# Attention decode with a gated MLP: VectorE's next product ahead of its last step on the maxima, and K's buffer signalled from an earlier matmul

## The chip, the cores and the metric

The kernel runs on one core of a Trainium2 chip. The metric is the device time in microseconds (us); lower is better. Engines are TensorE (PE, with its weight loads as PEld), VectorE (DVE), ScalarE (ACT), GpSimd (POOL) and SyncE (SP), which issues nearly all transfers. Data come from HBM through 16 DMA engines.

## The reference

One decoding step for two tokens with a long K and V cache, beside a small MLP whose output gates the attention's. All in float32.

```python
B, Sq, D = 2, 1, 512;  H, Sk, Dh = 32, 8192, 128;  F = 1376
xn = layernorm(x)
q = (xn @ wq)                                   # (B, H, 1, Dh)
scores = einsum("bhqd,bhkd->bhqk", q, k_cache) * Dh ** -0.5
o = einsum("bhqk,bhkd->bhqd", softmax(scores), v_cache)
s = o.reshape(B, 1, H * Dh) @ wo
h = gelu(layernorm(xn) @ w1 + b1)
g = silu(h @ w2 + b2)
return x + s * g
```

K and V are 2 x 32 heads x 8192 x 128 float32 each, so some 537 MB are read, against a few MB of weights.

## The kernel before, in words

Each of the 64 (token, head) heads has an 8192 x 128 K and V. Two heads make one **pair**: 64 partitions each, 128 rows of the cache on every partition. So there are N = 32 pairs, numbered 0 to 31, and a pair's K or V is one transfer of 128 x 16384 float32, 8 MiB. Three buffers of that size fill the memory: `KBUF[0]` and `KBUF[1]` for K by turns, and one `VB` for V. (All three carry the name `big` in the profile.) The weights of the set-up and at the end the output weights `wo` lie in the same buffers.

For each pair n:

- VectorE waits for the pair's q row (`s_q`, two accumulators in PSUM by turns) and for K (`d_k0` or `d_k1`), and multiplies K in place by q: the **product** (`TENSOR_TENSOR big<-big,bank`). It sums each row into 128 scores a partition: `TENSOR_REDUCE sc<-big`. The **maxima** of each partition come next: `TENSOR_REDUCE MX<-sc`, signal `v_mx`.
- TensorE transposes the row of maxima (`bank<-ident,MX`, signal `p_m`), and VectorE's **last step**, `TENSOR_REDUCE nm<-bank`, takes the largest of each head with its sign turned (signal `v_nm`).
- TensorE spreads the two numbers over the partitions with two small matmuls (`bank<-nm,srow`). The first gives K's buffer back (`p_k`), the second (`p_n`) sends ScalarE on: it copies the bias, takes two exponentials into `PZ` (signal `s_pz`) and writes the q of two pairs later (`s_q`).
- The **V stage**: TensorE waits for `s_pz` and for V (`d_v`), then runs 32 matmuls with V (`bank<-big,PZ`), ScalarE copies the result to `o4`, and eight matmuls collect it. The first of them gives `VB` back (`p_free`).
- `unread(...)` are matmuls whose results nobody reads; some stand between the others on TensorE.

SP issues transfers in an order written out by hand. In the middle it takes `p_k` and issues the K of two pairs later, then takes `p_free` and issues the next V, in turn, so that the queue holds K, V, K, V. The last K, the last V and `wo` are cut into pieces. On each engine a loop over the pairs (two to a turn on VectorE, ScalarE and SP) runs by itself, and `take` (line 45) is a wait on a semaphore that also counts it down. Most instructions of the program are recorded by one helper, so that they carry line 51.

At the start, K0 is loaded early, K1 after the q projection has been read from its buffer, and V0 once the whole set-up is done.

Of the kernel before, what the change touches and what calls it, by code (L numbers as in the profile page):

```python
# [5 lines left out]
ALU = mybir.AluOpType  # L6
AX = mybir.AxisListType
# [6 lines left out]
class Program:  # L14
# [28 lines left out]
    def take(self, eng, name, v=1):  # L43

        self.engines[eng].wait_ge(self.sem(name), v).then_inc(self.sem(name), -v)  # L45

    def op(self, eng, method, *args, waits=(), sig=None, by=1, quiet=False, **kwargs):
        need = self.need(eng, waits)
        for name, v in need[:-1]:
            self.engines[eng].wait_ge(self.sem(name), v)  # L50
        ins = getattr(self.engines[eng], method)(*args, **kwargs)  # L51
        for name, v in need[-1:]:
            ins._wait_ge(self.sem(name), v)
        if quiet:
            return None
        name = sig or "own_" + eng
        by = 16 if method == "dma_start" else by
        ins.then_inc(self.sem(name), by)
        self.counts[name] += by
        return name, self.counts[name]  # L60


def decode_kernel(nc, x, kc, vc, wq, wo, w1, b1, w2, b2, out):
    P = 128
    B, H, S, DH = kc.shape
# [3 lines left out]
    U = 2  # L69
    HP = P // U  # L70
    KP = S // HP
# [21 lines left out]
    HALVES = (0, KP // 2, KP)  # L93

    pr = Program(nc)
    op, wait, take = pr.op, pr.wait, pr.take

    def sb(shape, name):
        return nc.alloc_sbuf_tensor(name, list(shape), F32).ap()

    def ps(shape, name):
        return nc.alloc_psum_tensor(name, list(shape), F32).ap()
# [6 lines left out]
    KBUF, VB = rows[:2], rows[2]  # L109
# [24 lines left out]
    Q = sb([P, N + U, DH], "Q")  # L134
    ident = sb([P, P], "ident")
    ones = sb([P, B], "ones")
    srow = sb([1, HP], "srow")
# [18 lines left out]
    SC = [sb([P, KP], f"sc{i}") for i in range(2)]  # L156
    MX = sb([P, 1], "MX")
    nm = sb([1, U], "nm")
# [11 lines left out]
    bank = [ps([P, 512], f"bank{i}") for i in range(8)]  # L170
    po = bank[0]
    pm = bank[1]
    pn = bank[1][:, 2 * P:]
# [4 lines left out]
    pq2 = [bank[2][:, :DH], bank[7][:, :DH]]  # L178
# [8 lines left out]
    QH = len(PB) // 2  # L187
# [6 lines left out]
    def pe_n(name, n):  # L194
        return name, n + 1

    t = {}
# [31 lines left out]
    for k in (7, 6, 1, 2, 4, 0):  # L229
# [13 lines left out]
                  op=ALU.add)  # L243
    t["sel"] = op("DVE", "tensor_copy",
                  sel[:, HP:].rearrange("p (b j r) -> p b j r", b=B, r=HG)[:, :, :QT, 0], by_row[:, :B, :],
                  waits=[t["sel0"]])
# [36 lines left out]
    for part, n0, n1 in (("first", 0, NPB), ("rest", NPB, N)):  # L283
        shape = [BH, n1 - n0, DH]
        t[f"QN {part}"] = op("DVE", "tensor_tensor", out=QN[:, n0:n1, :], in0=q_all.unsqueeze(1).to_broadcast(shape),
                           in1=mine[:, n0:n1].unsqueeze(2).to_broadcast(shape), op=ALU.mult,
                           waits=[t["qall"], t["mine"]])
# [15 lines left out]
    for b in range(B):  # L303
        t["x4"] = op("SP", "dma_start", x4[HB * b::R, :], x[b, 0].rearrange("(j n) -> j n", n=P), sig="d_x4",
                     waits=[t["x4m"]])
# [23 lines left out]
            op("SP", "dma_start", wo_sb[:, c0:c1, n0:n1], wo_v[:, c0:c1, n0:n1], sig=f"d_wo{i}" if not h else "d_wol")  # L329


    def scores(u, q, sems, cuts):
        k = KBUF[u]
        for name, (c0, c1) in zip(sems, zip(cuts, cuts[1:])):
            take("DVE", name, 16)
            op("DVE", "tensor_tensor", out=k[:, c0:c1], in0=k[:, c0:c1],
               in1=q.unsqueeze(1).to_broadcast([P, c1 - c0, DH]), op=ALU.mult, sig="v_t")
            take("DVE", "v_t")
            op("DVE", "tensor_reduce", out=SC[u][:, c0:c1], in_=k[:, c0:c1], axis=AX.X, op=ALU.add, sig="v_r")
        take("DVE", "v_r", len(sems))  # L340
        op("DVE", "tensor_reduce", out=MX, in_=SC[u], axis=AX.X, op=ALU.max, sig="v_mx")
        take("DVE", "p_m")
        op("DVE", "tensor_reduce", out=nm, in_=pm[:1, :P].rearrange("o (s r) -> o s r", s=U), axis=AX.X,
           op=ALU.max, negate=True, sig="v_nm")

    with nc.vector.Fori(0, N // U - 1) as i:
        for u in range(U):
            take("DVE", "s_q")
            scores(u, pq2[u], [f"d_k{u}"], (0, KP))
    for u in range(U):  # L350
        take("DVE", "s_q")
        scores(u, pq2[u], ["d_k1", "d_kl"] if u else ["d_k0"], HALVES if u else (0, KP))


    with nc.scalar.Fori(0, N // U) as i:
        for u in range(U):
# [4 lines left out]
            for s in range(U):  # L361
# [11 lines left out]
                   waits=[t["th"], t["pool"]])  # L373
    shape = [P, N, U * PH]
    t["ZL"] = op("DVE", "tensor_tensor", out=ZL, in0=half.unsqueeze(1).to_broadcast(shape),
                 in1=RS.unsqueeze(2).to_broadcast(shape), op=ALU.mult, waits=[pe_n("p_z", 0), t["half"]])
# [3 lines left out]
                in1=OT.unsqueeze(2).to_broadcast(shape), op=ALU.mult, waits=[t["OT"], t["blk"]])  # L380
    t["on"] = op("DVE", "tensor_tensor", out=on[:, ::HB, :], in0=OA[:, :, :OC], in1=rl.unsqueeze(2).to_broadcast([P, B, OC]),
                 op=ALU.mult, waits=[t["rl"], t["on0"], pe_n("p_oa", 0)])
    t["wide"] = op("ACT", "copy", o4, pw, waits=[pe_n("p_w", 0)])
    a = op("DVE", "scalar_tensor_tensor", res, acc, 0.5, gate, op0=ALU.mult, op1=ALU.mult,
           waits=[pe_n("p_acc", 0), t["gate"]])
    t["res"] = op("DVE", "tensor_add", res, res, x4, waits=[a, t["x4"]])
    t["out"] = op("SP", "dma_start", out.rearrange("b s (j n) -> j (b s) n", n=P), res[::HB, :], sig="d_out",
                  waits=[t["res"]])
# [6 lines left out]
    def mm(dst, w, v, start=True, stop=True, sig=None, waits=(), skip=False):  # L395
        kw = {"skip_group_check": True} if skip else {}
        if sig in PE_EVENTS:
            done.append(sig)
            sig = "pe_setup"
        return op("PE", "matmul", dst, w, v, start=start, stop=stop, waits=waits, sig=sig, quiet=sig is None, **kw)  # L400
# [15 lines left out]
    for c in range(ND):  # L416
# [4 lines left out]
        j, k = NF % QT, NF // QT  # L421
# [6 lines left out]
    j, k = NF % QT, NF // QT  # L428
    mm(ph[R * j:R * j + B, k * P:k * P + FT], ones[:1, :B], b1_sb[:, NF * P:], start=False, stop=True, sig="ph")
    by_tile = ident.rearrange("p (j r) -> p j r", r=R)  # L430
    for k in range(NH):
        n = min(QT, NF + 1 - k * QT)
        mm(phT[:, k * QT * B:(k * QT + n) * B].rearrange("p (j b) -> p j b", b=B), h_nat[:, k * P:(k + 1) * P],
           by_tile[:, :n, :B], waits=[t["h"]], sig="phT" if k == NH - 1 else None)
    for n in range(NG // QT):
        for c in range(ND):
            for j in range(QT):
                g = n * QT + j
# [3 lines left out]
    for n in range(NG // QT):  # L442
        for hh in range(HG):
# [3 lines left out]
               waits=[t["sel"], t["qnat"]], sig="pqa" if last else None)  # L447

    for g in range(N // NPB):
        mm(PB[g % len(PB)], sides, QN[:, g * NPB:(g + 1) * NPB, :].rearrange("h n d -> h (n d)"),  # L450
           waits=[t["side"], t["QN rest" if g else "QN first"]] + ([t[f"Q{QH}"]] if g >= len(PB) else []),
           sig=f"pb{g}")
    for f in range(NF + 1):
        j = f % QT
        k = P if f < NF else FT
        mm(pg[R * j:R * j + B, :], hT[:k, f, :], w2_sb[:k, f, :], start=f < QT, stop=f + QT > NF and j != QT - 1,
           waits=[t["hT"], t["w2"], t["mem6"]])
    mm(pg[R * (QT - 1):R * (QT - 1) + B, :], ones[:1, :B], b2_sb, start=False, stop=True, waits=[t["b2"]], sig="pg")
    for j in range(QT):
        mm(pgate[R * j:R * j + MB, :], mod_b[:, :MB], g_nat[:, j * P:(j + 1) * P], waits=[t["g"], t["mod_b"]],  # L460
           sig="pgate" if j == QT - 1 else None)
    assert done == PE_EVENTS, done

    def unread(*heads):

        for n in heads:
            mm(bank[6][:, :n * DH], ident, Q[:, :n, :].rearrange("p n d -> p (n d)"), waits=[t["g"], t[f"Q{QH}"]])

    def softmax(first=False):
        if not first:  # L470
            unread(4, 4)
        take("PE", "v_mx")
        op("PE", "transpose", pm[:1, :P], MX, ident, sig="p_m")
        if not first:
            unread(1)
        take("PE", "v_nm")
        for s in range(U):
            mm(pn[HP * s:HP * (s + 1), :1], srow, nm[:, s:s + 1], sig="p_n" if s == U - 1 else "p_k")

    def weighted(v, last=False):  # L480
        if last:
            unread(4, 2)
        take("PE", "s_pz")
        if not last:
            take("PE", "d_v", 16)
        for i in range(NT):
            if last and i * JW == HALVES[1]:
                unread(2)
            if last and i * JW in HALVES:
                nc.tensor.wait_ge(pr.sem(f"d_v31{HALVES.index(i * JW)}"), 16)  # L490
            j = i % QT
            mm(po[R * j:R * j + U * JW, :], PZ[:, i].rearrange("p s j -> p (s j)"),
               v[:, i * JW:(i + 1) * JW, :].rearrange("p j d -> p (j d)"), start=i < QT, stop=i + QT >= NT,
               sig="p_v" if i == NT - 1 else "p_z" if last and i == 0 else None)
        if last:
            for b in range(B):
                m = slice(b * HH, (b + 1) * HH)
                mm(OA[:, b, OC:], ZL[:, m].rearrange("p n r -> p (n r)"), ones[:, :1], waits=[t["ZL"]],
                   sig="p_den" if b == B - 1 else None)
            unread(1)  # L500
        take("PE", "s_o4")
        for i in range(JW):
            mm(pt[:, :U], o4[:, i * DH:(i + 1) * DH], mod[:, i:U * JW:JW], start=i == 0, stop=i == JW - 1,
               sig="p_t" if i == JW - 1 else "p_free" if i == 0 else None)

    wait("PE", t["mem"], t["pool"], t["mod"], t["z"])
    softmax(first=True)
    with nc.tensor.Fori(0, N - 1):
        weighted(VB)
        softmax()  # L510
# [15 lines left out]
    for b in range(B):  # L526
        h = slice(b * H, (b + 1) * H)
        mm(OA[:, b, :OC], Z[:, h].rearrange("p h r -> p (h r)"), mod, waits=[t["Z"]],
           sig="p_oa" if b == B - 1 else None)
    unread(1)  # L530
    for i, (c0, c1) in enumerate(zip(WO_CUTS, WO_CUTS[1:])):
        for c in range(c0, c1):
            after = [t["on"], t["mem"], (f"d_wo{i}", 16)]
            if c < WIDE:
                j = c % QT
                mm(pw[R * j:R * j + MB, :], on[:, :, c], wo_sb[:, c, :], start=c < QT, stop=c + QT >= WIDE,
                   waits=after, sig="p_w" if c == WIDE - 1 else None)
# [7 lines left out]
        if c1 == OC - 2:  # L545
            for j in range(QT):
                mm(acc[R * j:R * j + MB, :], mod[:, :MB], o4[:, j * P:(j + 1) * P], start=False, stop=False,
                   waits=[t["wide"]])
# [26 lines left out]
```

## Time and profile before

| | |
|---|---|
| median of 3 runs | 1300.71 us (1299.7 to 1301.15) |
| the profiled execution's own time | 1299.53 us |
| its span, first to last instruction | 1298.2 us |
| VectorE busy | 1135.7 us, 87% |
| TensorE busy | 465.6 us, 36% |
| ScalarE busy | 81.1 us, 6% |
| moved from HBM | 559.30 MB, 431 GB/s over the span |

Busy times are sums over the span. The profile's numbers are those of one execution, whose time differs a little from the median.

### The profile page before, as it was taken

How to read it: one execution, taken by the hardware profiler on the slowest of the kernel's cores; microseconds unless marked ns; L12 is line 12 of the kernel's file. 1: busy time of each engine (PE TensorE's matmuls, PEld its weight loads, DVE VectorE, ACT ScalarE, POOL GpSimd, SP SyncE). 2: the span in 40 equal slices, each digit the busy share in tenths (PEclk: the TensorE clock that was granted, in tenths of full speed). 3: DMA queues.
4: the chain of work that ended last, by engine and by line, in shares of the span. 5: the costliest groups of instructions: out<-in, count | busy, mean ns of one | idle time of the engine just before them, and what ended most of it. 6: DMA issues, size and time to landing. Idle time of an engine off the chain costs nothing. (4 is left out here: it accounts for less than half of the span.)

```text
span 1298.2 us, 7420 instructions
## 1 busy us (share of the span) xinstructions
PE 465.6 (36%) x2958; PEld 150.8 (12%) x2958; DVE 1135.7 (87%) x171; ACT 81.1 (6%) x279; POOL 2.3 (0%) x15
## 2 busy tenths in 40 slices
PE   3813343323334322433322343322334321333338
PEld 1201111001111000111100111100111100111103
DVE  2599999988889988889988888988888988888991
ACT  1200000000000000000000000000000000000000
POOL 0000000000000000000000000000000000000000
PEclk8757766666776566677656767656776666677659
DMA  9999999999999999999999999999999999999998
GB/s 412 436 426 442 430 430 436 426 446 426 438 430 424 446 426 442 430 430 436 426 446 426 438 430 424 446 426 444 428 432 434 426 446 426 438 430 424 432 436 360
DMA packets 11241, 559.37 MB, mean 431 GB/s; under 512 B 1264, under 2 KB 1536, under 8 KB 1892
## 3 DMA queue, kind: packets, MB, share of 16 engines
q1 hardware_dynamic: 11228, 559.30, 99.7%
q8 instruction: 3, 0.05, 0.0%
q14 instruction: 2, 0.02, 0.0%
q10 hardware_dynamic: 8, 0.01, 0.0%
HBM read 559.30 MB, written 0.00 MB: 431 GB/s over the span
## 5 line engine op out<-in xcount | busy, mean ns | idle before, releaser
L51 DVE TENSOR_TENSOR big<-big,bank 128x16384 f32<-128x16384 f32 (+1 forms) x33 | 551.2, 16704 | 73.2 <-DVEq L45 73.2
L51 DVE TENSOR_REDUCE sc<-big 128x128 f32<-128x16384 f32 (+1 forms) x33 | 551.2, 16703 | 4.8
L51 PE MATMUL bank<-big,PZ 128*8 128x512 f32 x2048 | 293.0, 736 | 632.1 <-PEq L45 632.1
L51 PEld LDWEIGHTS bank<-big,PZ 128*8 128x8 f32 x2048 | 60.5, 103 | 837.3 <-issue 837.3
L51 PE MATMUL bank<-Q,ident 128*128 128x512 f32 (+2 forms) x198 | 79.8, 514 | 0.3 <-issue 0.3
L51 ACT COPY o<-bank 128x512 f32<-128x512 f32 x33 | 19.3, 586 | 887.3 <-ACTq L45 875.9
L51 PE MATMUL bank<-ident,MX 128*1 128x128 f32 x32 | 9.8, 308 | 132.8 <-PEq L45 132.8
L51 PE MATMUL bank<-mod,o 128*128 128x2 f32 x256 | 32.8, 250 | 27.4 <-PEq L45 27.4
L51 PEld LDWEIGHTS bank<-mod,o 128*128 128x128 f32 x256 | 31.0, 191 | 55.4 <-issue 55.4
L51 PEld LDWEIGHTS bank<-Q,ident 128*128 128x128 f32 x198 | 34.8, 205 | 16.5 <-issue 16.5
L51 ACT ACTIVATE PZ<-sc,bias 64x128 f32<-64x128 f32 x64 | 25.5, 399 | 6.6 <-ACTq L45 6.2
L51 DVE TENSOR_REDUCE nm<-bank 1x2 f32<-1x128 f32 x32 | 8.9, 279 | 19.4 <-DVEq L45 19.4
L51 DVE TENSOR_TENSOR big<-big,mine 64x512 f32<-64x512 f32 (+1 forms) x2 | 4.5, 2278 | 21.2 <-ACT big L51 21.2
L51 PEld LDWEIGHTS bank<-ident,MX 128*1 128x1 f32 x32 | 2.5, 79 | 157.8 <-issue 157.8
L51 ACT COPY bias<-bank 128x1 f32<-128x1 f32 x32 | 5.1, 159 | 220.2 <-ACTq L45 220.2
L51 PE MATMUL bank<-big,sides 64*128 64x512 f32 x16 | 12.8, 972 | 3.7 <-DVE big L51 3.7
L51 PE MATMUL bank<-nm,srow 1*64 1x1 f32 x128 | 10.4, 218 | 8.9 <-PEq L45 7.1
L51 DVE TENSOR_REDUCE MX<-sc 128x1 f32<-128x128 f32 x32 | 9.2, 286 | 4.7
L51 PE MATMUL bank<-big,xnT 128*2 128x512 f32 x64 | 9.0, 727 | 10.3 <-DMA big<-in_A_wq_dram 10.3
L51 ACT ACTIVATION_READ_ACCUMULATOR PZ<-sc,bias x64 | 11.8, 185 | 0.0
L51 PE MATMUL bank<-big,on 128*17 128x512 f32 (+1 forms) x88 | 10.8, 569 | 0.9 <-DMA big<-in_A_wo_dram 0.8
L51 DVE SCALAR_TENSOR_TENSOR res<-bank,gate 128x128 f32<-128x128 f32 x1 | 0.3, 291 | 11.9 <-PE bank L51 11.9
(80 smaller groups left out, 83.8 us busy)
## 6 DMA issues: line engine op xcount, KB each, us to landing
big<-in_A_k_cache_dram SPq DMA_DIRECT2D x2, 4096.0 KB, 35.9
big<-in_A_v_cache_dram SPq DMA_DIRECT2D x2, 4096.0 KB, 35.8
big<-in_B_w_dram SPq DMA_DIRECT2D x1, 2752.0 KB, 10.2
big<-in_B_w_dram SPq DMA_DIRECT2D x1, 2560.0 KB, 52.1
big<-in_A_wo_dram SPq DMA_DIRECT2D x1, 2560.0 KB, 15.0
big<-in_A_wo_dram SPq DMA_DIRECT2D x1, 2048.0 KB, 19.5
big<-in_A_wo_dram SPq DMA_DIRECT2D x1, 1536.0 KB, 22.7
big<-in_A_wo_dram SPq DMA_DIRECT2D x1, 1024.0 KB, 24.8
```

Of the source, the lines that this page charges most:

```text
L51: ins = getattr(self.engines[eng], method)(*args, **kwargs)
```

## The change

On VectorE the function `scores`, which did all steps of one pair, is cut into `product`, `total`, `maxima` and `largest`. The product of pair n+1 now stands between the maxima of pair n and the last step of pair n; the wait for K of pair n+1 stands ahead of it, so ahead of that last step too. The first product stands ahead of the loop. In the last pair the two halves are kept in their order.

On TensorE the signal `p_k`, which gives K's buffer back, moves from the first small matmul with `nm` to the matmul of no use between the transpose and the wait for `v_nm`. The first pair now has that matmul too.

```diff
-    def scores(u, q, sems, cuts):
-        k = KBUF[u]
-        for name, (c0, c1) in zip(sems, zip(cuts, cuts[1:])):
-            take("DVE", name, 16)
-            op("DVE", "tensor_tensor", out=k[:, c0:c1], in0=k[:, c0:c1],
-               in1=q.unsqueeze(1).to_broadcast([P, c1 - c0, DH]), op=ALU.mult, sig="v_t")
-            take("DVE", "v_t")
-            op("DVE", "tensor_reduce", out=SC[u][:, c0:c1], in_=k[:, c0:c1], axis=AX.X, op=ALU.add, sig="v_r")
-        take("DVE", "v_r", len(sems))
+    def product(u, name, c0=0, c1=KP):
+        take("DVE", name, 16)
+        op("DVE", "tensor_tensor", out=KBUF[u][:, c0:c1], in0=KBUF[u][:, c0:c1],
+           in1=pq2[u].unsqueeze(1).to_broadcast([P, c1 - c0, DH]), op=ALU.mult, sig="v_t")
+
+    def total(u, c0=0, c1=KP):
+        take("DVE", "v_t")
+        op("DVE", "tensor_reduce", out=SC[u][:, c0:c1], in_=KBUF[u][:, c0:c1], axis=AX.X, op=ALU.add, sig="v_r")
+
+    def maxima(u, n=1):
+        take("DVE", "v_r", n)
         op("DVE", "tensor_reduce", out=MX, in_=SC[u], axis=AX.X, op=ALU.max, sig="v_mx")
+
+    def largest():
         take("DVE", "p_m")
         op("DVE", "tensor_reduce", out=nm, in_=pm[:1, :P].rearrange("o (s r) -> o s r", s=U), axis=AX.X,
            op=ALU.max, negate=True, sig="v_nm")
 
+    take("DVE", "s_q")
+    product(0, "d_k0")
     with nc.vector.Fori(0, N // U - 1) as i:
         for u in range(U):
+            total(u)
+            maxima(u)
             take("DVE", "s_q")
-            scores(u, pq2[u], [f"d_k{u}"], (0, KP))
...
+            product(1 - u, f"d_k{1 - u}")
+            largest()
+    total(0)
+    maxima(0)
+    take("DVE", "s_q")
+    product(1, "d_k1", *HALVES[:2])
+    largest()
+    total(1, *HALVES[:2])
+    product(1, "d_kl", *HALVES[1:])
+    total(1, *HALVES[1:])
+    maxima(1, 2)
+    largest()
...
         op("PE", "transpose", pm[:1, :P], MX, ident, sig="p_m")
-        if not first:
-            unread(1)
+        unread(1, sig="p_k")
         take("PE", "v_nm")
         for s in range(U):
-            mm(pn[HP * s:HP * (s + 1), :1], srow, nm[:, s:s + 1], sig="p_n" if s == U - 1 else "p_k")
+            mm(pn[HP * s:HP * (s + 1), :1], srow, nm[:, s:s + 1], sig="p_n" if s == U - 1 else None)
```

VectorE, from the last instruction of the set-up through the first product and one turn of the loop (two pairs; `-` before, `+` after):

```order
 L51 TENSOR_TENSOR big<-big,mine 64x3584
-L346 UNCONDITIONAL_BRANCH
 L51 TENSOR_TENSOR big<-big,bank 128x16384
+L352 UNCONDITIONAL_BRANCH
 L51 TENSOR_REDUCE sc<-big 128x128
 L51 TENSOR_REDUCE MX<-sc 128x1
+L51 TENSOR_TENSOR big<-big,bank 128x16384
 L51 TENSOR_REDUCE nm<-bank 1x2
-L51 TENSOR_TENSOR big<-big,bank 128x16384
 L51 TENSOR_REDUCE sc<-big 128x128
```

The product of the next pair (`TENSOR_TENSOR big<-big,bank`) has moved ahead of the last step of this one (`nm<-bank`), from the very first pair on.

TensorE, in the first pair, from the set-up's last matmuls to the V stage that opens the loop:

```order
 L51 MATMUL bank<-big,mod_b 17x128 x4
 L51 MATMUL bank<-ident,MX 1x128
+L51 MATMUL bank<-Q,ident 128x128
 L51 MATMUL bank<-nm,srow 64x1 x2
-L508 UNCONDITIONAL_BRANCH
+L524 UNCONDITIONAL_BRANCH
 L51 MATMUL bank<-big,PZ 8x512 x32
```

Between the transpose (`bank<-ident,MX`) and the matmuls with `nm` stands one more matmul; it carries the signal for K's buffer, in this pair and in all others. The V stage (`bank<-big,PZ`) stays behind the matmuls with `nm`. SP's order is the same before and after.

## Rows read from the trace of the kernel before

**Rows 1.** Page, parts 1 and 2: busy shares, transfer rate in 40 slices, bytes.

```profile
PE 465.6 (36%) x2958; PEld 150.8 (12%) x2958; DVE 1135.7 (87%) x171; ACT 81.1 (6%) x279; POOL 2.3 (0%) x15
...
GB/s 412 436 426 442 430 430 436 426 446 426 438 430 424 446 426 442 430 430 436 426 446 426 438 430 424 446 426 444 428 432 434 426 446 426 438 430 424 432 436 360
DMA packets 11241, 559.37 MB, mean 431 GB/s; under 512 B 1264, under 2 KB 1536, under 8 KB 1892
```

**Rows 2.** Timeline, middle: start us, us, engine, operation, count, [idle before].

```profile
520.81 9.82 PE L51 MATMUL bank<-big,PZ 128*8 128x512 f32 x64 [21.76 <-PEq L45]
...
532.03 0.33 SPq L51 DMA_DIRECT2D big<-in_A_v_cache_dram  x1
...
536.77 0.64 PE L51 MATMUL bank<-Q,ident 128*128 128x128 f32 x2
...
537.55 0.38 PE L51 MATMUL bank<-nm,srow 1*64 1x1 f32 x4
...
538.15 0.33 SPq L51 DMA_DIRECT2D big<-in_A_k_cache_dram  x1
...
540.15 17.22 DVE L51 TENSOR_TENSOR big<-big,bank 128x16384 f32<-128x16384 f32 x1 [2.75 <-DVEq L45]
...
559.51 9.24 PE L51 MATMUL bank<-big,PZ 128*8 128x512 f32 x64 [21.58 <-PEq L45]
...
570.23 0.33 SPq L51 DMA_DIRECT2D big<-in_A_v_cache_dram  x1
...
578.85 17.22 DVE L51 TENSOR_TENSOR big<-big,bank 128x16384 f32<-128x16384 f32 x1 [2.83 <-DVEq L45]
```

**Rows 3.** List of issues (median us to landing), list of waits (total, times, longest).

```profile
big<-in_A_k_cache_dram SPq DMA_DIRECT2D x31, 40.7
...
DVE big L51 <- DVEq L45: 73.2, 28, 2.8
```

**Rows 4.** The chain that ended last, in order of time: start us, us, what.

```profile
1268.40 25.56 DMA big<-in_A_wo_dram
```

**Rows 5.** Timeline, first pairs, VectorE, TensorE and SP.

```profile
85.01 0.29 DVE L51 TENSOR_REDUCE MX<-sc 128x1 f32<-128x128 f32 x1
...
86.23 17.22 DVE L51 TENSOR_TENSOR big<-big,bank 128x16384 f32<-128x16384 f32 x1
...
95.09 9.35 PE L51 MATMUL bank<-big,PZ 128*8 128x512 f32 x64 [8.32 <-PEq L45]
...
105.92 0.34 SPq L51 DMA_DIRECT2D big<-in_A_v_cache_dram  x1
...
133.79 8.77 PE L51 MATMUL bank<-big,PZ 128*8 128x512 f32 x64 [11.07 <-PEq L45]
...
172.51 9.89 PE L51 MATMUL bank<-big,PZ 128*8 128x512 f32 x64 [13.55 <-PEq L45]
...
269.24 17.22 DVE L51 TENSOR_TENSOR big<-big,bank 128x16384 f32<-128x16384 f32 x1 [2.79 <-DVEq L45]
```

**Rows 6.** Timeline, last pairs.

```profile
1178.74 8.54 PE L51 MATMUL bank<-big,PZ 128*8 128x512 f32 x64 [21.76 <-PEq L45]
...
1188.62 0.34 SPq L51 DMA_DIRECT2D big<-in_A_v_cache_dram  x1
...
1269.99 0.28 DVE L51 TENSOR_REDUCE nm<-bank 1x2 f32<-1x128 f32 x1 [0.57 <-DVEq L45]
...
1272.43 3.62 PE L51 MATMUL bank<-big,PZ 128*8 128x512 f32 x32
```

**Rows 7.** Issues list; windows (busy times, clock, DMA share, GB/s); timeline, the end.

```profile
big<-in_B_w_dram SPq DMA_DIRECT2D x1, 192.0 KB, 4.1
...
1.40:1.60 0.20, 0.00 (x0) 0.00 (x0) 0.14 (x2) 0.00 (x0) 0.20 (x2) 1.00 0.00 0
1.60:1.80 0.20, 0.00 (x0) 0.00 (x0) 0.20 (x1) 0.00 (x0) 0.20 (x2) 1.00 0.72 133
...
1296.49 0.63 SPq L51 DMA_DIRECT2D out_dram<-res  x1
```

More of the change, by code (lines that the diff above doesn't have):

```diff
@@ L344, in scores @@
            op=ALU.max, negate=True, sig="v_nm")
+    take("DVE", "s_q")
+    product(0, "d_k0")
     with nc.vector.Fori(0, N // U - 1) as i:
         for u in range(U):
+            total(u)
+            maxima(u)
             take("DVE", "s_q")
-            scores(u, pq2[u], [f"d_k{u}"], (0, KP))
-    for u in range(U):
-        take("DVE", "s_q")
-        scores(u, pq2[u], ["d_k1", "d_kl"] if u else ["d_k0"], HALVES if u else (0, KP))
+            product(1 - u, f"d_k{1 - u}")
[10 more added lines that the diff above has]
+    largest()
     with nc.scalar.Fori(0, N // U) as i:
@@ L462, in decode_kernel, with unread @@
     assert done == PE_EVENTS, done
-    def unread(*heads):
+    def unread(*heads, sig=None):
         for n in heads:
-            mm(bank[6][:, :n * DH], ident, Q[:, :n, :].rearrange("p n d -> p (n d)"), waits=[t["g"], t[f"Q{QH}"]])
+            mm(bank[6][:, :n * DH], ident, Q[:, :n, :].rearrange("p n d -> p (n d)"), waits=[t["g"], t[f"Q{QH}"]],
+               sig=sig)
     def softmax(first=False):
```

## The prediction

> **What bounds the kernel now.** I read the page's busy shares and its row of transfer rates first, then the timeline of a stretch in the middle, then the start, then the chain that ended last.
>
> VectorE is busy for 87% of the span, which looks like the bound. But the rate row stands between 412 and 446 GB/s in every slice up to the last one, with 559.37 MB moved at a mean of 431 [rows 1]. So two resources are nearly full, and the timeline has to say which waits for which.
>
> In the middle, a pair's product starts at 540.15 and the next at 578.85 [rows 2]: a period of 38.70 us, in which one K and one V (8 MiB each) arrive. That is 19.35 us a transfer, and 2 x 8.389 MB / 38.70 us = 433.5 GB/s. VectorE stands idle for 2.75 and 2.83 us ahead of these products. What it waits for there: the K issued at 538.15 takes 40.7 us (median, [rows 3]) to land, and 538.15 + 40.7 = 578.85 is the start of that product. That K was issued 2.0 us before the K ahead of it landed (540.15), and behind it the V issued at 532.03, whose landing lets TensorE begin at 559.51. 540.15 + 19.35 = 559.50, and 559.50 + 19.35 = 578.85. So transfers run one behind the other in SP's order, without a gap, and each buffer is asked for ahead of its turn: K by 559.5 - 538.15 = 21 us, V by 578.85 - 570.23 = 8.6 us. VectorE's idle time is waiting for a full queue; 73.2 us of it come in 28 waits [rows 3]. The chain that ended last is 25.56 us of the output weights' transfer and some 4 us behind it [rows 4]. All 559.37 MB at 433.5 GB/s are 1290.4 us of the 1298.2. Whatever the engines save is lost on the next transfer, and the only thing that moves the end is a moment at which the queue runs empty.
>
> **The first pairs are another stage.** Products start late here, since the set-up of Q comes first, and VectorE runs behind the transfers: product 1 at 86.23 has no idle time ahead of it, and 2.79 us are seen only ahead of the product at 269.24 [rows 5]. The waits for a V are the clock of the queue here: TensorE begins on V0 at 95.09, on V1 at 133.79, on V2 at 172.51 [rows 5], again 38.70 apart. So K2 lands at 133.79 - 19.35 = 114.44, and V1, issued at 105.92, is asked for 8.5 us ahead of its turn.
>
> **The change, part by part.** No operation goes and none is added but one 128x128 matmul of no use behind the first transpose, of the kind that takes 0.64 us for two passes [rows 2]. TensorE stands idle for 8.32 us behind that place [rows 5], which covers it; without that cover it would cost 0.64 us once.
>
> *K given back earlier.* The signal moves from the first small matmul (537.55) to the one on the matmul behind the transpose (536.77): 0.8 us earlier a pair [rows 2]. K is asked for 21 us ahead already, so it's worth nothing. The SP queue takes p_k and p_free in the old order; a K issued earlier doesn't pass a V.
>
> *Product ahead of the last step, middle pairs.* The product waits for K until 540.15 as now and ends at 557.37. Only then comes the last step on the maxima, which before stood ahead of K's landing. Queued behind it are TensorE's small matmul, ScalarE's bias and exponentials, and the V stage. From that step's start to the V stage with its data there, pair 31 shows 1269.99 to 1272.43, 2.44 us [rows 6]. So the V stage may start at 557.37 + 2.44 = 559.81 and not at 559.51, when V lands: 0.3 us late. VB is given back that much later, and 0.3 of the 8.6 us of lead are used. Cost nothing; were the lead gone it would be 0.3 us a pair, 28 pairs, 8 us.
>
> *The same move at pair 0.* Here K1 has long landed and the product doesn't wait: it starts when the maxima are done, 85.01 + 0.29 = 85.30, and runs 17.22 us [rows 5]. The last step of pair 0, before the change right ahead of the product at 86.23, starts at 102.52. V0's stage follows at 102.52 + 2.44 = 104.96 and not at 95.09, when V0 lands: 9.87 us late, over the 8.5 us of lead. From that stage's start to the issue of the next V the trace has 95.09 to 105.92 = 10.83 us for this very pair [rows 5], and elsewhere from 9.88 (1178.74 to 1188.62) to 11.22 (520.81 to 532.03) [rows 2, 6]; I take 10.83. V1 is issued at 104.96 + 10.83 = 115.79 (114.84 to 116.18). K2 is in at 114.44. The queue runs empty.
>
> *What an empty queue costs.* V1 lands at its issue + L + 19.35, where L is the time from issue to landing that isn't transfer and that a full queue hides. The trace has no transfer that finds the queue empty in the middle, so I bound L. From below: the result's 4 KB are issued at 1296.49 [rows 7] and the span ends at 1298.2, so 1.7 us. From above: the kernel's first transfer, 192 KB, lands 4.1 us after issue; 0.45 us of that is its data at 433.5 GB/s, so 3.65 [rows 7]. The first shares the start with other queues; the other runs alone, as V1 would, but has few descriptors. I take 2.0, near the lower. Bytes of the first transfer are seen between 1.6 and 1.8, 0.9 to 1.1 us after its issue at 0.74 [rows 7], so L can't be under that.
>
> The Trainium skill (DMA: Bandwidth & Descriptors, section Specifications) gives a first-byte latency of about 0.6 us for transfers issued from SP. By that figure alone the standstill would be 115.79 + 0.6 - 114.44 = 1.95 us, within what a measurement can't tell; the trace doesn't agree, with 0.9 us or more to the first bytes.
>
> The loss: 115.79 + 2.0 - 114.44 = **3.35 us**, with bounds 114.84 + 1.7 - 114.44 = 2.1 and 116.18 + 3.65 - 114.44 = 5.4. It can't be won back, since every later transfer stands behind it in a full queue.
>
> *Pair 1 and on.* Product 2 would start at about 120.4 (102.52 + 0.28 + 17.22 + 0.4 for the maxima), so pair 1's last step comes at 137.6, its V stage at 140.1, and V2's issue at 150.9. K3 now lands at 172.51 - 19.35 = 153.16, and behind the gap at 156.5. V2 is 5.6 us ahead: no second gap (each V would have to come over 5 us later still). From product 3 (K3 at 156.5) VectorE waits for K, as in the middle.
>
> *The end.* K31 comes in two halves, so pair 30's last step moves behind half a product only. In the middle the whole product makes the V stage 0.3 us late; with half of 17.22 us, the step comes some 8 us before V30's stage needs it. Pair 31 keeps its order. Nothing there moves but by the 3.35 us, and the output weights stay the last transfer.
>
> **Sum.** The profiled execution took 1299.53 us around its span of 1298.2; + 3.35 = 1302.9. The median of the three runs is 1300.71, 1.2 above, and a comparison goes by medians: 1300.71 + 3.35 = **1304.1**, 0.26% slower. A difference under 0.2% (2.6 us) can hardly be told from none here.
>
> **Rivals.**
>
> *The standstill is short.* Were L 1.0 us, what the first bytes show, the loss would be 115.79 + 1.0 - 114.44 = 2.35 us: 1303.1, no measurable change. So it is with the V stage of 9.88 and L = 2.0: 114.84 + 2.0 - 114.44 = 2.4. For it: the bounds reach there. Against: a landing is seen only after the last byte, and the 4 KB row has 1.7 in all. The Trainium skill's 0.6 us would end in this case. The point from which it decides is an issue plus L under 117.0.
>
> *Faster: VectorE's order is the bound after all.* It is idle 2.8 us a pair, and the product now needn't wait for the last step. If K's issue set K's landing, 0.8 us of earlier issue on 28 waits would give 22 us: 1278. For it: VectorE at 87% and the 73.2 us of waits. Against: K is issued while the queue is busy with two transfers ahead, and every slice moves over 410 GB/s up to the last. It decides only if K's lead of 21 us were under 0.
>
> *Slower by more: a second gap.* If V2 too came late (5.6 us of lead) or the V stage grew by over 6 us in the middle, each gap would cost about another 3 us: 1307 and up. No row has a V stage over 11.22.
>
> **Chances.** One gap of over 2.6 us, as forecast: 0.62, with a range of its own from 1302.8 to 1306.1. Short gap or none: 0.28. More than one gap: 0.06. Faster: 0.04. The range leaves out the faster case, the many gaps and the extreme of the last: 1300.7 (no gap) to 1306.4. Slower 0.68, same 0.28, faster 0.04.
>
> **What would show it.** In the profile of the changed kernel: V0's stage starts near 105.0 and V1's issue stands near 115.8, behind K2's landing; V1's stage begins near 137.2 at the earliest and only there a 2 to 5 us hole in the rate; product 4 and later are 38.70 apart as before, each about 3.4 us later; V stages in the middle start some 0.3 us behind V's landing; the chain still ends on the output weights. I am wrong if V1 is issued before 114.4, if the hole is under 2.6 us, or if the period differs from 38.70.

## The result, and the profile after

The changed kernel takes 1305.19 us (median of 5 runs, 1304.7 to 1306.32) beside 1300.04 us for the kernel before on the same chip: a ratio of 1.004, 95% interval 1.0029 to 1.0051. It is slower by 5.15 us, 0.4%, small but outside the noise. Forecast were 1304.1 us, with 1300.7 to 1306.4, and slower as the likeliest.

The profiled execution took 1304.70 us around a span of 1302.6. Against the span of before (1298.2) 4.4 us lie inside, and the other 0.8 of this pair of executions lie around the span (2.1 in place of 1.3 us).

The page, with its first two parts and VectorE's product from part 5:

```profile
PE 464.2 (36%) x2960; PEld 150.6 (12%) x2960; DVE 1131.6 (87%) x171; ACT 81.0 (6%) x279; POOL 2.3 (0%) x15
...
GB/s 410 435 425 386 427 443 419 451 419 451 419 451 419 449 421 443 427 429 441 419 451 419 451 419 451 419 451 419 441 429 433 437 421 449 419 451 419 434 435 356
...
L51 DVE TENSOR_TENSOR big<-big,bank 128x16384 f32<-128x16384 f32 (+1 forms) x33 | 551.2, 16704 | 102.3 <-DVEq L45 102.3
```

Compared with [rows 1], the shares are the same. In the rate row one slice stands out, the fourth, 386 GB/s in place of 442; a slice is 32.6 us, so it covers 97.7 to 130.3. VectorE's wait ahead of its products has grown from 73.2 to 102.3 us, which alone would mislead: in the middle the last step, and the wait ahead of it, have left the stretch before the product, and their time is now booked to the wait for K.

The first pairs, beside [rows 5] (start us, length us, engine, operation):

```profile
85.45 17.22 DVE L51 TENSOR_TENSOR big<-big,bank 128x16384 f32<-128x16384 f32 x1
...
102.58 0.27 DVE L51 TENSOR_REDUCE nm<-bank 1x2 f32<-1x128 f32 x1
...
105.15 8.53 PE L51 MATMUL bank<-big,PZ 128*8 128x512 f32 x64 [1.77 <-PEq L45]
...
115.17 0.34 SPq L51 DMA_DIRECT2D big<-in_A_v_cache_dram  x1
...
120.44 17.22 DVE L51 TENSOR_TENSOR big<-big,bank 128x16384 f32<-128x16384 f32 x1
...
140.13 9.81 PE L51 MATMUL bank<-big,PZ 128*8 128x512 f32 x64 [1.76 <-PEq L45]
...
156.59 17.22 DVE L51 TENSOR_TENSOR big<-big,bank 128x16384 f32<-128x16384 f32 x1 [1.13 <-DVEq L45]
```

The product of pair 1 starts at 85.45, the last step of pair 0 follows at 102.58, and V0's stage at 105.15 instead of 95.09. V1 is issued at 115.17 instead of 105.92. The windows say whether the queue was empty then. Their columns are length, then busy times of PE, PEld, DVE, ACT and POOL, TensorE's granted clock (as a share of full speed), DMA share and GB/s; a packet counts where it begins. First the kernel before, then the changed kernel:

```profile
112.00:113.00 1.00, 0.00 (x0) 0.00 (x0) 1.00 (x1) 0.00 (x0) 0.00 (x0) 1.00 1.82 786
113.00:113.50 0.50, 0.00 (x0) 0.00 (x0) 0.50 (x1) 0.00 (x0) 0.00 (x0) 0.92 0.30 131
...
114.00:116.00 2.00, 0.00 (x0) 0.00 (x0) 2.00 (x1) 0.00 (x0) 0.00 (x0) 0.50 0.98 426
```

```profile
112.00:116.00 4.00, 3.12 (x26) 1.43 (x19) 4.00 (x1) 0.74 (x2) 0.00 (x0) 1.00 0.00 0
116.00:116.50 0.50, 0.50 (x3) 0.26 (x2) 0.50 (x1) 0.00 (x0) 0.00 (x0) 1.00 4.70 1573
```

Before, packets begin in every window shown, and V1's follow K2's without a gap. In the changed kernel no packet with data begins between 112 and 116 us; by the trace K2's last one, of 64 KB, ends at 114.06, and V1's first begins at 116.15. Then 12 of the 16 DMA engines begin within half a microsecond (1573 GB/s in one window are 12 packets of 64 KB), and the other four by 117.1.

How long it was: V1's stage now waits for ScalarE, so V1's landing is read from what is behind it in the queue. Product 3 starts at 156.59 on K3's landing, so V1 landed at 156.59 - 19.35 = 137.24. From its issue that is 137.24 - 115.17 - 19.35 = 2.72 us without data.

The middle, beside [rows 2]:

```profile
543.63 17.22 DVE L51 TENSOR_TENSOR big<-big,bank 128x16384 f32<-128x16384 f32 x1 [3.68 <-DVEq L45]
...
563.32 9.84 PE L51 MATMUL bank<-big,PZ 128*8 128x512 f32 x64 [1.76 <-PEq L45]
...
574.63 0.33 SPq L51 DMA_DIRECT2D big<-in_A_v_cache_dram  x1
...
582.32 17.22 DVE L51 TENSOR_TENSOR big<-big,bank 128x16384 f32<-128x16384 f32 x1 [3.68 <-DVEq L45]
```

The period is 38.70 us as before. The V stage starts 0.3 us behind V's landing (543.63 + 19.35 = 562.98), and V is issued 7.7 us ahead of K's landing. The product at 578.85 before is the one at 582.32 now: 3.47 us late. That is the hole and 0.2 us that the set-up took longer.

The end, first before, then after: the product of pair 30 and the stage of pair 30's V.

```profile
1198.10 17.22 DVE L51 TENSOR_TENSOR big<-big,bank 128x16384 f32<-128x16384 f32 x1 [2.84 <-DVEq L45]
...
1256.22 9.05 PE L51 MATMUL bank<-big,PZ 128*8 128x512 f32 x64 [21.64 <-PEq L45]
```

```profile
1201.52 17.22 DVE L51 TENSOR_TENSOR big<-big,bank 128x16384 f32<-128x16384 f32 x1 [3.69 <-DVEq L45]
...
1260.54 9.39 PE L51 MATMUL bank<-big,PZ 128*8 128x512 f32 x64 [14.64 <-PEq L45]
```

The first is 3.42 us late, the second 4.32. Between these two rows stood 58.12 us and now stand 59.02, though both wait for transfers that follow one another in the queue. So a second, smaller delay of 0.9 us exists, at the end. The chain that ended last is still the output weights:

```profile
1273.05 25.25 DMA big<-in_A_wo_dram
```

It ends at 1298.30 instead of 1293.96, 4.3 us later, and that is the difference of the spans.

### The profile page after: what moved, and what is told of

Its sections match the earlier page's. It is cut to its first block, busy times and chain, and to the rows that moved or that the text cites. A ratio compares the mean times of both kernels' runs of the same rounds, so it can differ in the third digit from the quotient of the medians.

```text
span 1302.6 us, 7424 instructions
## 1 busy us (share of the span) xinstructions
PE 464.2 (36%) x2960; PEld 150.6 (12%) x2960; DVE 1131.6 (87%) x171; ACT 81.0 (6%) x279; POOL 2.3 (0%) x15
## 5 line engine op out<-in xcount | busy, mean ns | idle before, releaser
L51 DVE TENSOR_TENSOR big<-big,bank 128x16384 f32<-128x16384 f32 (+1 forms) x33 | 551.2, 16704 | 102.3 <-DVEq L45 102.3
L51 PEld LDWEIGHTS bank<-nm,srow 1*64 1x64 f32 x128 | 10.1, 197 | 621.6 <-issue 621.6
```

## The experiments

Theory A is the prediction's: one standstill of the queue behind pair 0. Theory B: every pair's later V stage, or VectorE's order itself, costs a little.

**Pair 0 in the old order.** VectorE's loop now begins at pair 1; all other pairs keep the new order.

```diff
     product(0, "d_k0")
+    total(0)
+    maxima(0)
+    largest()
+    take("DVE", "s_q")
+    product(1, "d_k1")
...
-        for u in range(U):
+        for u in (1, 0):
```

Expected: 

> Changed kernel, but pair 0 does its last step ahead of product 1, as before; all other pairs keep the new order. Theory A (the loss is one standstill of the queue, because V0's stage and so V1's issue come late at pair 0): V1 is asked for near 105.9 again and its hole is gone. Pair 1 now has the same trouble, smaller: its V stage starts near 141.0 (138.45 + 2.44 and a little), V2 is issued at 149.6 to 152.3, K3 lands near 153.1; with 2.6 us from issue to landing without data, as V1 showed in the changed kernel, that leaves 0 to 1.8 us: 1300.0 to 1301.8. Theory B (the loss comes from every pair's later V stage): 30 of 31 pairs are left, so still 1305.

Measured: 1302.2 us, ratio 1.0017 (1.0008 to 1.0026).

```profile
106.06 0.34 SPq L51 DMA_DIRECT2D big<-in_A_v_cache_dram  x1
...
141.05 8.63 PE L51 MATMUL bank<-big,PZ 128*8 128x512 f32 x64 [1.76 <-PEq L45]
...
151.07 0.33 SPq L51 DMA_DIRECT2D big<-in_A_v_cache_dram  x1
...
193.18 17.22 DVE L51 TENSOR_TENSOR big<-big,bank 128x16384 f32<-128x16384 f32 x1 [1.37 <-DVEq L45]
```

The hole behind K2 is gone: V1 is issued at 106.06. Pair 1 now has the late V stage, at 141.05, and V2 is issued at 151.07. That is 2.1 us ahead of K3's landing, and still V2 comes late: product 4 at 193.18 puts its landing at 173.83, where 151.07 + 19.35 = 170.42, so 3.4 us without data, and 1.3 us behind the 172.51 of [rows 5]. Being asked for before the landing isn't enough; the lead must also cover the start of a transfer and the spread of the engines. The trace shows why: the 16 DMA engines don't end a transfer together. The first is through with K3 at 150.84, 2.3 us ahead of the landing, and 13 of the 16 by 151.8, but V2's first packet begins at 152.04, 1.0 us behind its issue. So engines stand idle though the queue is never quite empty. V2's first packets then take 2.6 to 3.3 us where later ones take 2.4. The time is above the range of theory A by 0.4 us, so that range was missed, and far under theory B's.

**Pairs 0 and 1 in the old order.** The same, with both pairs taken out of the loop.

Expected: 

> Changed kernel, but pairs 0 and 1 in the old order, 2 to 30 in the new. Theory A: pair 2's V stage starts near 177.3, V3 is issued near 188 against K4's landing near 191.8, so no hole anywhere: within 0.5 us of the kernel before, 1300.0. Theory B: 29 of 31 pairs are left, about 1304.9.

Measured: 1300.32 us, ratio 1.0004 (0.9995 to 1.0013). With 29 pairs in the new order no loss can be told. Theory B is out.

```profile
187.81 0.33 SPq L51 DMA_DIRECT2D big<-in_A_v_cache_dram  x1
```

This V3, asked for 4.0 us ahead of K4's landing (191.8), lands at 211.1, as it did before: a lead of 4 us is enough.

**Only pair 0 in the new order.**

```diff
-    with nc.vector.Fori(0, N // U - 1) as i:
-        for u in range(U):
-            total(u)
-            maxima(u)
-            take("DVE", "s_q")
-            product(1 - u, f"d_k{1 - u}")
-            largest()
+    total(0)
+    maxima(0)
+    take("DVE", "s_q")
+    product(1, "d_k1")
+    largest()
...
```

Expected: 

> Only pair 0 in the new order, with the earlier signal for K; pairs 1 to 31 in the old order. Theory A: the whole loss, 3.3 to 5.3 us over the kernel before, with the hole behind K2. Theory B: one pair of 31, under 0.3 us.

Measured: 1304.68 us, ratio 1.0039 (1.0025 to 1.0052): the whole loss from one pair.

```profile
106.15 8.41 PE L51 MATMUL bank<-big,PZ 128*8 128x512 f32 x64 [1.77 <-PEq L45]
...
116.05 0.34 SPq L51 DMA_DIRECT2D big<-in_A_v_cache_dram  x1
...
138.20 9.45 PE L51 MATMUL bank<-big,PZ 128*8 128x512 f32 x64 [15.46 <-PEq L45]
...
177.61 2.75 PE L51 MATMUL bank<-big,PZ 128*8 128x512 f32 x12 [18.75 <-PEq L45]
```

V1's stage starts at 138.20 on its landing; 138.20 - 116.05 - 19.35 = 2.80 us without data. The next stage comes 39.41 us later, where 38.70 would be two transfers: the smaller delay, 0.7 us, stands here at pair 2 and not at the end.

**The signal alone.** The kernel before, with `p_k` on the matmul behind the transpose.

Expected: 

> The kernel before, with the signal for K's buffer moved to the matmul behind the transpose, and nothing else. Theory A: K is issued some 0.5 to 0.9 us earlier in each pair, lands when it did, no change within 0.5 us. Theory C (the earlier issue of K disturbs the V in flight): part of the 5 us shows here. If the issue set the landing, 22 us would be gained.

Measured: 1300.09 us, ratio 1.0001 (0.9992 to 1.001).

```profile
537.53 0.28 DVE L51 TENSOR_REDUCE nm<-bank 1x2 f32<-1x128 f32 x1 [0.57 <-DVEq L45]
537.85 0.33 SPq L51 DMA_DIRECT2D big<-in_A_k_cache_dram  x1
...
540.64 17.22 DVE L51 TENSOR_TENSOR big<-big,bank 128x16384 f32<-128x16384 f32 x1 [2.83 <-DVEq L45]
...
579.33 17.22 DVE L51 TENSOR_TENSOR big<-big,bank 128x16384 f32<-128x16384 f32 x1 [2.83 <-DVEq L45]
```

K is issued 0.32 us behind the start of the last step, in place of 1.0 us, so 0.7 us earlier, and the next product still starts 38.69 us after this one. Theory C is out, and so is a landing that the issue sets.

**Half a product ahead.** Each product in two instructions, the last step between them.

```diff
-            product(1 - u, f"d_k{1 - u}")
+            part(1 - u, *HALVES[:2], f"d_k{1 - u}")
             largest()
+            part(1 - u, *HALVES[1:])
```

Expected: 

> Changed kernel with each product (of 128 x 16384) cut into two instructions of 128 x 8192, and the last step between them: only 8.7 us of VectorE's work stand ahead of it, in all pairs. Theory A: pair 0's last step comes near 94.1, its V stage near 96.6, V1 is asked for near 107.4, 7 us ahead of K2's landing; pair 1's V stage no longer comes behind V1's landing. No hole, 1300.0 within 0.7 us. Theory B (any work and the wait for K ahead of the last step costs in every pair): at least half of the 5 us stays, 1302.5.

Measured: 1299.86 us, ratio 1.0 (0.9991 to 1.0009).

```profile
93.94 0.27 DVE L51 TENSOR_REDUCE nm<-bank 1x2 f32<-1x128 f32 x1
...
107.29 0.34 SPq L51 DMA_DIRECT2D big<-in_A_v_cache_dram  x1
...
133.81 6.42 PE L51 MATMUL bank<-big,PZ 128*8 128x512 f32 x36 [3.84 <-PEq L45]
```

V1 is issued at 107.29, 7 us ahead of its turn, and its stage starts at 133.81, as before. The new order costs nothing when only half as much work stands ahead of the last step. It also wins nothing.

**The old signal under the new order.**

```diff
-        unread(1, sig="p_k")
+        if not first:
+            unread(1)
         take("PE", "v_nm")
         for s in range(U):
-            mm(pn[HP * s:HP * (s + 1), :1], srow, nm[:, s:s + 1], sig="p_n" if s == U - 1 else None)
+            mm(pn[HP * s:HP * (s + 1), :1], srow, nm[:, s:s + 1], sig="p_n" if s == U - 1 else "p_k")
```

Expected: 

> Changed kernel with K's signal back at its old place, behind the last step. Theory A with 2.6 to 3.3 us from issue to landing without data: at pair 0 K2 is issued near 103.6 where its turn is at 95.0, a hole of some 11 us. In the middle K is issued 18.0 us after the other K landed, 1.3 us ahead of its turn, which isn't enough: a period of 18.0 + 2.6 to 3.3 + 19.35 = 40.0 to 40.6 us in place of 38.70, on some 29 pairs. In all 1349 to 1367. Theory D (any issue ahead of the landing is early enough): only the hole at the start, about 1311.

Measured: 1353.96 us, ratio 1.0409 (1.0395 to 1.0424).

```profile
103.55 0.36 SPq L51 DMA_DIRECT2D big<-in_A_k_cache_dram  x1
...
125.63 17.22 DVE L51 TENSOR_TENSOR big<-big,bank 128x16384 f32<-128x16384 f32 x1 [5.21 <-DVEq L45]
...
143.76 0.33 SPq L51 DMA_DIRECT2D big<-in_A_k_cache_dram  x1
...
165.87 17.22 DVE L51 TENSOR_TENSOR big<-big,bank 128x16384 f32<-128x16384 f32 x1 [5.22 <-DVEq L45]
```

K2 is issued at 103.55, with its turn at 95.0, and lands at 125.63, 11.2 us late. From there each K is issued 18.1 us behind the other K's landing, 1.2 us ahead of its turn, and the period is 40.24 us. 165.87 - 143.76 - 19.35 = 2.76 us without data. Up to the product of pair 30, at 1250.40, the mean period is 40.17, 1.47 over 38.70, so 11.2 + 29 x 1.47 = 53.8 us would be the loss; 53.9 was measured. Theory D is out. The moved signal, worth nothing by itself, is what keeps the new order from costing ten times as much.

**Pair 0's V stage late by other means.** The kernel before, with matmuls of no use in front of the first V stage.

```diff
     softmax(first=True)
+    unread(*[4] * 16)
```

Expected with 16: 

> The kernel before, with 16 matmuls of 512 columns whose results nobody reads in front of pair 0's V stage alone, VectorE's order untouched. They take some 14 us from 86.8 on, so the V stage starts near 100.7 and V1 is issued near 109.3 to 110, still 4.5 to 5 us ahead of K2's landing at 114.4. Theory A: no loss, 1300.0 within 0.7 us. Theory E (any delay of the V stage is lost): 1305.

Measured: 1301.55 us, ratio 1.0011 (1.0002 to 1.002).

```profile
111.34 0.34 SPq L51 DMA_DIRECT2D big<-in_A_v_cache_dram  x1
...
134.35 6.14 PE L51 MATMUL bank<-big,PZ 128*8 128x512 f32 x36 [11.35 <-PEq L45]
```

The matmuls took longer than I had counted, so V1 was issued at 111.34, 3.3 us ahead of its turn (K2 lands at 114.60 here). In the profiled execution, whose time was the lowest of the eleven (1300.09), V1's stage comes 0.56 us later than before; 0.29 of that is a later set-up and 0.27 the queue's. The median lost 1.5 us, above what theory A was said to give and far under theory E's 5. The expectation of no loss was for 4.5 us of lead; with 3.3 the case isn't the one that was forecast, and it stands near the edge that the first experiment found.

Expected with 28: 

> As the run with 16, with 28 such matmuls: V stage near 111.2, V1 issued near 119.7. Theory A: a loss of 119.7 + 2.6 - 114.4 = 7.9 us and up to 0.9 more: 1308 to 1309. Theory B (the order of VectorE itself costs the time): no loss, since VectorE keeps its old order.

Measured: 1311.19 us, ratio 1.0087 (1.0073 to 1.01).

```profile
121.34 0.34 SPq L51 DMA_DIRECT2D big<-in_A_v_cache_dram  x1
...
143.36 6.89 PE L51 MATMUL bank<-big,PZ 128*8 128x512 f32 x40 [18.81 <-PEq L45]
```

V1 is issued at 121.34, its stage starts at 143.36: 2.67 us without data, 9.6 us later than before. VectorE's order is the old one. A late V stage at pair 0 alone makes the loss, and its size follows the issue.

**V given back earlier, beside the changed kernel again.** `p_free` moves to one more matmul right behind the V stage.

Expected: 

> Changed kernel with V's buffer given back right behind the V stage's last matmul (by one more matmul that nobody reads), not behind ScalarE's copy of the result and the next matmul. Theory A: V1 is issued some 0.9 us earlier, near 114.3 in place of 115.17, and the hole shrinks from 3.3 to about 2.4 us: 1304.2 against the changed kernel's 1305.2. Theory B (late V stages cost by themselves): 1305, since V stages start when they did.

For the changed kernel: 

> The changed kernel once more, beside the one with V given back early. 1304.7 to 1306.3 again; V1's stage some 3.2 to 4.5 us later than before, as its V stage at pair 0 takes from 8.5 to 9.9 us, and the extra lag of 0.7 to 0.9 us somewhere behind it.

Measured: 1304.89 us, ratio 1.0035 (1.0021 to 1.0048), and 1304.73 us, ratio 1.0039 (1.0025 to 1.0053). First V given back early, then the changed kernel:

```profile
105.54 9.74 PE L51 MATMUL bank<-big,PZ 128*8 128x512 f32 x64 [1.77 <-PEq L45]
...
115.95 0.34 SPq L51 DMA_DIRECT2D big<-in_A_v_cache_dram  x1
```

```profile
105.25 8.35 PE L51 MATMUL bank<-big,PZ 128*8 128x512 f32 x64 [1.78 <-PEq L45]
...
115.08 0.34 SPq L51 DMA_DIRECT2D big<-in_A_v_cache_dram  x1
```

The issue comes 0.67 us behind the V stage's last matmul (105.54 + 9.74 to 115.95) in place of 1.48, as meant. But the stage itself took 9.74 us here and 8.35 there, and the 0.8 us went into that. The medians are the same, and this one decides nothing between the theories. It shows how large a part the V stage's own length has in the hole.

**The last K uncut.** For the smaller delay at the end; the last product is then one instruction too.

Expected: 

> Changed kernel with the last K as one transfer and one product in place of two halves. In the changed kernel 58.12 us between the product of pair 30 and the V stage of pair 30 (before) have become 59.02, beside the hole of 3.3 us. Theory F (the two halves cause the extra 0.9 us when the transfers start in step behind a hole): 58.1 again. Theory G (the lag has another cause, and shows wherever it meets engines in step): 0.7 to 0.9 us extra stay, here or at another pair. The end of the kernel may be later, since pair 31's scores come 4 us later; only the two times are compared.

Measured: 1305.13 us, one run.

```profile
1202.73 17.22 DVE L51 TENSOR_TENSOR big<-big,bank 128x16384 f32<-128x16384 f32 x1 [3.69 <-DVEq L45]
...
1242.30 17.22 DVE L51 TENSOR_TENSOR big<-big,bank 128x16384 f32<-128x16384 f32 x1 [4.55 <-DVEq L45]
```

39.57 us between two products that both wait for K, where two transfers take 38.70: the 0.87 us are there with K uncut. Theory F falls.

What the runs with the delay have in common is found in the list of queues. Once in the middle of every run, one 8 KB packet of another queue, q14 (instructions), is booked. In the run with only pair 0 changed it comes at 161.60 us, while V2's delay is made:

```profile
q14 instruction: 1, 0.01, 0.2%
```

In the changed kernel it comes at 1222.61, while K31 arrives. In the kernel before it comes at 1219.27, while K31 arrives there too, and costs nothing: 58.12 us between the two rows of the end.

The traces show the difference. Everywhere but in the run with the old signal, where the packet comes between two transfers, one DMA engine (its packets followed from the end of one to the begin of the next) loses 0.3 us to the packet, and its next packet of K or V takes 0.5 to 0.7 us longer than all others (2.42 us for 64 KB, 1.22 for 32 KB). So this engine falls 0.8 to 1.0 us behind. Whether that counts depends on the other 15: the traces have the landing 0.3 to 0.5 us behind the end of the transfer's last engine. Here is the round of 16 packets behind the one that was held up, first with only pair 0 changed, then with pairs 0 and 1 in the old order, where no hole went before and the packet comes at 160.82:

```profile
163.60:164.35 0.75, 0.00 (x0) 0.00 (x0) 0.75 (x1) 0.00 (x0) 0.00 (x0) 0.50 3.02 1311
164.35:165.50 1.15, 0.00 (x0) 0.00 (x0) 1.15 (x1) 0.00 (x0) 0.00 (x0) 0.50 0.13 57
```

```profile
163.95:164.35 0.40, 0.00 (x0) 0.00 (x0) 0.40 (x1) 0.00 (x0) 0.00 (x0) 0.50 0.38 164
164.35:165.00 0.65, 0.00 (x0) 0.00 (x0) 0.65 (x1) 0.00 (x0) 0.00 (x0) 0.50 0.70 302
```

In the first, 15 packets begin in the upper window and the held-up engine's alone in the lower one, at 164.91: behind a hole all engines had begun at nearly the same time, so it's the last, and V2 lands 0.73 us late. In the second, the engines are spread over 1.7 us; the held-up one begins in the upper window, three others later still, and V2 lands on time.

So it is in the eleven traces that can tell: in the six with a hole of 3 us or more at V1 the transfer with the packet is late by 0.7 to 0.9 us, in the five without one by less than 0.1. In the first experiment the packet comes while V2 arrives, at 160.02, but the held-up engine isn't V2's last, so the packet has no part in the loss there. No run moved the packet on purpose. And smaller lags, of 0.1 to 0.4 us, come in two traces without any such packet (K31 uncut, V given back early); they stay open.

## Why the prediction was right, and where it was off

*The full queue as the bound: right.* The period stayed at 38.70 us with VectorE's order changed in every pair. The half-product kernel, with no hole, is at 1299.86.

*The signal alone worth nothing: right* (ratio 1.0001). What I didn't work out is what it is worth under the new order: 1353.96 - 1305.19 = 48.8 us.

*Late V stages in the middle cost nothing: right.* They start 0.3 us late, as forecast, with 7.7 us of lead left.

*The late V stage of pair 0: right in each step.* The last step was forecast at 102.52 and came at 102.58; V0's stage 104.96 and 105.15; V1's issue 115.79 and 115.17, since the V stage took 8.53 us and not the 9.35 it had there before. One pair makes the whole loss.

*What an empty queue costs, L = 2.0: mis-sized.* Read the same way, seven holes measure 2.55 to 2.80 (2.72 in the changed kernel's profile, 2.80 with only pair 0 changed, 2.67 with the delay of 28), and K under the old signal, with 1.2 us of lead, 2.76; all between the bounds 1.7 and 3.65. The short transfer at the end was the nearer row in surroundings but not in kind. In the profiled execution the earlier issue (-0.6) and the larger L (+0.7) cancel, and the hole costs 3.3 us (3.47 less the set-up's 0.2) where 3.35 was said: that this number came out so close is luck.

*"Nothing there moves but by the 3.35 us": wrong.* 0.9 us are lost once more at the end. The step that failed is that a hole costs its length and nothing else: it also leaves the DMA engines so close together that one engine, held up by the packet of q14, makes K31 0.9 us late.

*The time came closer than the loss.* 1304.1 was built on a median of 1300.71, from three runs; with five it is 1300.04. So 1305.19 is 1.1 us above the forecast, but the loss is 5.15 where 3.35 was said, and the range held it because it was wide. In the profiled pair, 0.2 (set-up) + 3.3 + 0.9 make the 4.4 us inside the span. The profiled execution has the shortest span of the changed kernel's five, 1302.6, and their median is 1303.9. In the further traces with the change at pair 0 the hole itself goes from 3.0 to 3.8 us with the length of V0's stage; where the others of the five lost their time no trace shows.

*The rivals.* The short standstill needed issue plus L under 117.0; it was 115.17 + 2.72 = 117.9. A second gap of the size thought of, from a late V2, didn't come: V2 was issued at 151.33, with K3 landing at 156.5. The faster case had no part.

The first experiment adds to the step on pair 1: its lead of 5.6 us was enough only because the first hole had moved K3. With pair 0 in the old order it is 2.1 us, and costs 2 us of time.

## What to carry to other kernels

Where transfers run one behind the other in a full queue, ask of each edit one question: which request for a transfer becomes late, and is it still ahead of the queue's end by the time that a transfer takes to start. Here 4.0 us of lead cost nothing and 3.3 us a little. Check it in the stage where the engines run behind the transfers too, not only in the steady one. The edit was harmless in 29 pairs and cost 5 us in the first, where VectorE was never waiting and the moved step really had to stand behind 17 us of work. A step that another engine waits for goes ahead of long work, or the long work is cut so that it fits between.

## What the runs showed of the hardware that was not expected

A transfer of 8 MiB that finds the queue empty loses 2.55 to 2.80 us from its issue until an engine starts on its landing, beside its 19.35 us of data (seven holes). In all seven its first packet begins 0.96 to 0.98 us after the issue. For V1 in the changed kernel the 16 engines begin from 0.98 to 1.92 us after it, their first packets take 2.5 to 3.5 us where later ones take 2.42, and the last engine begins its second packet 4.69 us after the issue. So 4.69 - 2.42 = some 2.3 us are gone by then, and only the last 0.35 lie between the last packet and the landing. The Trainium skill (DMA: Bandwidth & Descriptors, section Anatomy of one DMA) names a fixed cost of about 2.0 us for transfers issued from GpSimd, most of it at the end of the transfer. The trace, of transfers issued from SP, has 0.6 to 0.8 us more than that, and most of it at the start; for these the measurement decides.

A request that comes 2.1 us before the transfer ahead of it lands is already late: 1.3 us in the profiled execution with pair 0 in the old order, 2.2 us in its median. With 3.3 us it was 0.3 us in the trace (1.5 in the median), with 4.0 us nothing, and with 1.0 to 1.2 us, under the old signal, 1.5 us a pair.

One 8 KB packet of another queue sets one of the 16 engines back by 0.8 to 1.0 us. It cost 0.7 to 0.9 us of the whole when a hole had let all engines begin nearly together (the others end within 0.4 to 0.9 us of one another), and nothing when they were spread over 1.5 to 2.2 us.
